# A table set loaded by hand, a clamp moved to VectorE, and a re-timed plan in an attention and two-MLP kernel

## The chip, the cores and the metric

One core of a Trainium2 chip runs the whole program. The metric is the device time of one execution in microseconds, the median of several; lower is better.

## The reference

Three layers follow each other. Delta-rule attention keeps a 48x48 state per head, for 4 batches, 8 heads and 768 steps; its output, seen as 3072 tokens of 384, goes through a first Mlp with a rational function, and then through a second Mlp with Mish. Both Mlps have 2048 hidden units, and their weights come as float64.

```python
for t in range(S):
    y[:, :, t] = einsum('bhd,bhde->bhe', q_t, state)
    v_old = einsum('bhde,bhd->bhe', state, k_t)          # k_t is normalised
    state = state + b_t * einsum('bhd,bhe->bhde', k_t, v_t - v_old)
h = x @ w_in;  P = a0 + a1*h + a2*h**2 + a3*h**3
Q = 1 + |b0|*|h| + |b1|*h**2;  x = (P / (Q + 1e-6)) @ w_out     # first Mlp
h = x @ w_in2; out = (h * tanh(log1p(exp(h)))) @ w_out2           # second Mlp (Mish)
```

## The kernel before

**Stages.** Time is cut into 24 chunks of 32 steps, and four chunks make a group G of 512 tokens (G from 0 to 5). A group passes through: norms of k (`norms`), per chunk transposes and Gram products on PE (`prepare`), one triangular inverse for all four chunks (`inverse`: a VectorE transpose at L355, 30 elimination steps of a product L364 and a sum L370, a transpose back L374, a scaling L377), and four recurrent steps (`step`, one chunk each, whose second product at L431 needs the inverse `xt`). The inverse's 30 steps run on VectorE for G = 0 and on GpSimd (POOL) for G = 1 to 5 (`ONPOOL`). Then come 16 units of the first Mlp and 16 of the second, each unit a slice of 128 hidden columns: nine matmuls up (L639), an elementwise chain, nine matmuls down (L645). The stages follow one another as first Mlp G0, second Mlp G0, first G1, second G1, first G2, second G2, first G3, second G3, first G4, first G5, second G4, second G5. The steps of group G + 1 lie beside the second Mlp of group G, so the stage pairs carry attention work as well.

**The first Mlp's unit.** On ScalarE (ACT) it runs Abs (L665), Identity (L669, every other unit; else POOL does it at L667), Identity (L670), Ln (L674), Exp (L675) and a copy (L679); the quotient 1/Q is exp(-ln Q), improved by a Newton step on VectorE (DVE: L672, L673, L676 to L678). POOL multiplies at L671 and forms the low half at L680. The hidden tile `h` has two PSUM banks, so the up product of unit i + 2 waits until the chain of unit i has read its bank, at L673 last. The second Mlp's unit has two Mish activations (L682, L683) and one DVE subtraction (L684).

**Function tables.** One preload at the start of the program (L746) selects a set that holds both Ln and Exp. Everywhere else the table load in front of an activation is put there when the program is compiled, not by this code; it is seen in the trace as ACT_TABLE_LOAD with the line of the activation behind it.

**Weights.** 64 tiles of float64 weights (16 slices, two sides, two Mlps) are turned into pairs of float32 tiles and stored in a scratch in HBM, from which each unit fetches its slice (L632). A tile j goes through a load into `raw` (L532 to L543), a magnitude into `wm` (L549 on ACT, or L547 on DVE for the last 20), a clamp (L552), a shift, a sign and a low part on DVE (L557, L562, L567), a high half on ACT (L574), a low half on POOL (L577) and a store (L590). The clamp is on POOL for j below 24 and from 44 on, on DVE between. `raw`, `wm` and `st` have two buffers each.

**The plan.** No engine's order is written out. `Plan.add` takes every operation with an engine, a planned duration in ns, and the buffers that it reads and writes; `Plan.order` works back from the units' due times to a latest start of every operation, takes the operation's `early` off it, and then simulates the engines in time: whenever one is free it takes, among its operations that are ready, the one with the smallest value. The code is issued in that order, and each engine, and SP's queue of DMA issues with it, runs its own part strictly in that order. So planned durations and `early` values change no instruction, only the order; `AHEADX` is the `early` of the norms, of the copies and masks of `prepare` and of the whole inverse, and 0 before.

Of the kernel before, what the change touches and what calls it, by code (L numbers as in the profile page):

```python
# [23 lines left out]
START = 90000  # L24
AHEAD = 30000
AHEADP = 100000
AHEADX = 0
ONPOOL = (1, 2, 3, 4, 5)
LAG = 3.5
EARLY = 6  # L30
PER_KB = 3.3


# [93 lines left out]
class Attention:  # L127
# [222 lines left out]
    def inverse(self, p, G):  # L350
        nc, M, tmp, xt, xs = self.nc, self.M, self.tmp, self.xt, self.xs
        engine, eng = ("POOL", nc.gpsimd) if G in ONPOOL else ("DVE", nc.vector)

        def first():
            nc.vector.transpose(out=xs, in_=self.lg.rearrange("p u m s -> p s (u m)"))  # L355

        def diag():
            eng.memset(xs.rearrange("p a b -> p (a b)")[:, 0:C * C:C + 1], 1.0)

        def step(j):  # L360
            def f():
                n = C - 1 - j
                tv = tmp[:, 0:j * n].rearrange("p (c i) -> p c i", c=j)
                eng.tensor_tensor(  # L364
                    out=tv,
                    in0=xs[:, j, j + 1:C].unsqueeze(1).to_broadcast([128, j, n]),
                    in1=xs[:, 0:j, j:j + 1].to_broadcast([128, j, n]),
                    op=ALU.mult,
                )
                eng.tensor_tensor(out=xs[:, 0:j, j + 1:C], in0=xs[:, 0:j, j + 1:C], in1=tv, op=ALU.add)  # L370
            return f

        def last():
            nc.vector.transpose(out=xt.rearrange("p n t -> p t n"), in_=xs.rearrange("p j i -> p i j"))  # L374

        def scale():
            nc.gpsimd.tensor_tensor(  # L377
                out=xt, in0=xt,
                in1=self.beta_t[:, GU * G:GU * G + GU].rearrange("p u m -> p (u m)").unsqueeze(2).to_broadcast([128, GU * M, C]),
                op=ALU.mult,  # L380
            )

        p.add("DVE", 2000, first, [f"lg{g}" for g in range(GU)], ["xs"], early=AHEADX)
        p.add(engine, 160, diag, (), ["xs"], early=AHEADX)
        for j in range(1, C - 1):
            n = j * (C - 1 - j)
            p.add(engine, int(3.4 * n + 440) if engine == "POOL" else 2 * (n + 190), step(j), (), ["xs", "tmp"], early=AHEADX)
        p.add("DVE", 2070, last, ["xs"], ["xt"], early=AHEADX)
        p.add("POOL", 1950, scale, (), ["xt"], early=AHEADX)

    def step(self, p, u):
        nc, M, D = self.nc, self.M, self.D
# [100 lines left out]

        p.dma(8 * 400, 300, lambda: self.load_v(u), (), [vb], early=AHEAD)
        p.dma(1200, 200, swap, [knb], [knsb], early=AHEAD)
        p.add("PE", 850, ks, [kb, f"{sb}0", f"{sb}1"], [bc], early=AHEAD)
        p.add("DVE", 560, rest, [bc, vb], ["r2"], early=AHEAD)
        p.add("PE", 850, uu, ["r2", "xt"], [bc], early=AHEAD)
        p.add("ACT", 480, u_out, [bc], ["U"], early=AHEAD)
        if u + 1 < self.NU:  # L500
            for c in range(2):
                p.add("PE", 850, s_mm(c), ["U", knb, knsb], [bs[c]], early=AHEAD)
                p.add("DVE", 560, s_out(c), [bs[c], f"{sb}{c}"], [f"{tb}{c}"], early=AHEAD)
        p.add("PE", 2600, y_mm, [f"{sb}0", f"{sb}1", "U", qb, ab], [by], early=AHEAD)
# [6 lines left out]
class Weights:  # L511
# [8 lines left out]
        self.w_in = w_in  # L520
        self.w_out = w_out.rearrange("f (k c) -> f k c", c=128)

    def plan(self, p, f, side, j, late, pool):
        nc, bufs = self.nc, self.bufs
        raw, m, st = (bufs[n][j % len(bufs[n])] for n in ("raw", "wm", "st"))
        rawb, mb, stb = (f"{n}{j % len(bufs[n])}" for n in ("raw", "wm", "st"))
# [22 lines left out]
                nc.scalar.activation(out=m.bitcast(F32), in_=words[:, :, 1].bitcast(F32), func=ACTF.Abs)  # L549

        def size():
            (nc.gpsimd if pool else nc.vector).tensor_scalar(  # L552
                out=m.bitcast(F32), in0=m.bitcast(F32), scalar1=self.LEAST, scalar2=self.MOST, op0=ALU.max, op1=ALU.min,
            )

# [22 lines left out]

        p.dma(380 if side or self.n else 2500, 384, get, (), [rawb])
        if late:  # L580
            p.add("DVE", 600, mag, [rawb], [mb])
        else:
            p.add("ACT", 550, mag, [rawb, "table"], [mb])
        p.add("POOL" if pool else "DVE", 720 if pool else 450, size, (), [mb])
        p.add("DVE", 450, shift, (), [mb])
        p.add("DVE", 650, sign, [rawb], [mb])
        p.add("DVE", 650, low, [rawb], [mb])
        p.add("ACT", 510, hi, [mb], [stb])
        p.add("POOL", 1040, lo, [mb], [stb])
        p.dma(380, 384, lambda: nc.sync.dma_start(out=self.scratch[f][:, side], in_=st.bitcast(F32)), [stb], [f"wd{self.n}_{f}_{side}"])  # L590


class Mlps:
# [22 lines left out]
    def plan_unit(self, p, m, G, NG, f, nf, due):  # L616
# [41 lines left out]

        p.dma(330, 384, fetch(0, win), [f"wd{m - 1}_{f}_0"], [winb], early=6000)
        p.dma(330, 384, fetch(1, wout), [f"wd{m - 1}_{f}_1"], [woutb], early=6000)  # L660
        p.add("PE", 2050, up, [winb] + [f"X{b}_{j}" for j in range(GU)], [hb], due=due)
        act = nc.scalar.activation
        V, A, P = nc.vector, nc.scalar, nc.gpsimd
        if m == 1:
            p.add("ACT", 595, lambda: act(out=q, in_=h, func=ACTF.Abs), [hb], [qb])  # L665
            if i % 2:
                p.add("POOL", 810, lambda: P.tensor_scalar(out=r, in0=q, scalar1=k["b1"], scalar2=k["b0"], op0=ALU.mult, op1=ALU.add), [qb], [rb])  # L667
            else:
                p.add("ACT", 820, lambda: act(out=r, in_=q, func=ACTF.Identity, scale=k["b1"], bias=k["b0"]), [qb], [rb])  # L669
            p.add("ACT", 775, lambda: act(out=s, in_=h, func=ACTF.Identity, scale=k["a3"], bias=k["a2"]), [hb], [sb])  # L670
            p.add("POOL", 1335, lambda: P.tensor_tensor(out=q, in0=q, in1=r, op=ALU.mult), [rb], [qb])  # L671
            p.add("DVE", 680, lambda: V.tensor_tensor(out=s, in0=s, in1=h, op=ALU.mult), [hb], [sb])  # L672
            p.add("DVE", 750, lambda: V.scalar_tensor_tensor(out=s, in0=s, scalar=k["a1"], in1=h, op0=ALU.add, op1=ALU.mult), [hb], [sb])  # L673
            p.add("ACT", 2000 if first and G in (1, 2, 3, 4) else 690, lambda: act(out=r, in_=q, func=ACTF.Ln, bias=k["c"]), [qb], [rb] + (["table"] if first and G in (1, 2, 3, 4) else []))  # L674
            p.add("ACT", 580, lambda: act(out=rp, in_=r, func=ACTF.Exp, scale=-1.0), [rb, "table"], ["r"])  # L675
            p.add("DVE", 685, lambda: V.scalar_tensor_tensor(out=q, in0=q, scalar=1.0 + 1e-6, in1=rp, op0=ALU.add, op1=ALU.mult), ["r"], [qb])  # L676
            p.add("DVE", 750, lambda: V.scalar_tensor_tensor(out=rp, in0=s, scalar=k["a0"], in1=rp, op0=ALU.add, op1=ALU.mult), [sb], ["r"])  # L677
            p.add("DVE", 690, lambda: V.scalar_tensor_tensor(out=q, in0=q, scalar=2.0, in1=rp, op0=ALU.subtract, op1=ALU.mult, reverse0=True), ["r"], [qb])  # L678
            p.add("ACT", 625, lambda: A.copy(out=gh[:, 0], in_=q), [qb], [ghb])  # L679
            p.add("POOL", 1320, lambda: P.tensor_tensor(out=gh[:, 1], in0=q, in1=gh[:, 0].bitcast(F32), op=ALU.subtract), [qb], [ghb])  # L680
        else:
            p.add("ACT", 2000 if first and G < 5 else 600, lambda: act(out=gh[:, 0], in_=h, func=ACTF.Mish), [hb], [ghb] + (["table"] if first and G < 5 else []))  # L682
            p.add("ACT", 595, lambda: act(out=q, in_=h, func=ACTF.Mish), [hb, "table"], [qb])  # L683
            p.add("DVE", 700, lambda: V.tensor_tensor(out=gh[:, 1], in0=q, in1=gh[:, 0].bitcast(F32), op=ALU.subtract), [qb], [ghb])  # L684
        if m == 2 and G == NG - 1:
            rows = ["o0", "o1", "o2", "t0"]
            p.add("PE", 2100, down_rows, [woutb, ghb], rows, due=due + LAG * PACE)
# [36 lines left out]
def tile_delta_attention_two_mlps(  # L724
# [120 lines left out]
```

## Time and profile before

| | us |
|---|---|
| median of 3 runs (1470.32 to 1471.16) | 1470.34 |
| the profiled execution's own time | 1469.16 |
| its span, first to last instruction | 1467.4 |

| engine | busy, us | share of the span |
|---|---|---|
| PE (TensorE matmul) | 1139.7 | 78% |
| ACT (ScalarE) | 787.8 | 54% |
| DVE (VectorE) | 701.3 | 48% |
| POOL (GpSimd) | 635.2 | 43% |

Busy time is the time in which at least one instruction of the engine was running. A stage is a stretch between the first up products of two neighbouring groups of 16 units, read from the starts of L639. The granted clock is TensorE's clock as a share of full speed, so a PE that is busy at a low clock does less.

### The profile page before, as it was taken

How to read it: one execution, taken by the hardware profiler on the slowest of the kernel's cores; microseconds unless marked ns; L12 is line 12 of the kernel's file. 1: busy time of each engine (PE TensorE's matmuls, PEld its weight loads, DVE VectorE, ACT ScalarE, POOL GpSimd, SP SyncE). 2: the span in 40 equal slices, each digit the busy share in tenths (PEclk: the TensorE clock that was granted, in tenths of full speed). 3: DMA queues.
4: the chain of work that ended last, by engine and by line, in shares of the span. 5: the costliest groups of instructions: out<-in, count | busy, mean ns of one | idle time of the engine just before them, and what ended most of it. 6: DMA issues, size and time to landing. Idle time of an engine off the chain costs nothing.

```text
span 1467.4 us, 32391 instructions
## 1 busy us (share of the span) xinstructions
PE 1139.7 (78%) x13162; PEld 898.4 (61%) x13162; DVE 701.3 (48%) x1128; ACT 787.8 (54%) x1177; POOL 635.2 (43%) x743
## 2 busy tenths in 40 slices
PE   5048766578877778997788978889984897789986
PEld 4047544356665656775566766667763675568776
DVE  4874889776535542236632236532142655552211
ACT  2123665422258971259961279942273889992211
POOL 5453765696425573015672025770038434440000
PEclk9556988788888999998999998999997899999998
DMA  5755777766783644554644546553543344547562
GB/s 114 201 167 133 234 222 240 235 198 214 212 241 84 197 110 127 130 152 112 183 131 115 140 119 167 144 148 99 130 113 96 83 110 133 134 134 192 160 197 76
DMA packets 209285, 224.81 MB, mean 153 GB/s; under 512 B 134864, under 2 KB 147664, under 8 KB 209136
## 3 DMA queue, kind: packets, MB, share of 16 engines
q1 hardware_dynamic: 205616, 222.04, 54.6%
q8 instruction: 104, 1.70, 0.5%
q10 hardware_dynamic: 3264, 0.59, 0.2%
q14 instruction: 45, 0.37, 0.1%
q0 software_dynamic: 256, 0.10, 0.0%
HBM read 190.42 MB, written 29.88 MB: 150 GB/s over the span
## 4 chain that ended last, share of the span: by engine, by line
PE 31%; ACT 31%; POOL 13%; DVE 7%; DMA 6%; issue 6%; SPq 5%; ACTq 0%; DVEq 0%; POOLq 0%
PE b_h L639 11%; PE b_o L645 9%; ACT L675 6%; ACT L674 6%; POOL xs L370 5%; POOL tmp L364 4%; ACT mr L674 4%; ACT ms L670 3%; ACT b_r L675 3%; ACT mq L665 3%; ACT gh L679 2%; PE b_t L448 2%; SPq L712 2%; POOL wm L552 2%; DMA raw<-in_moe_w_in_dram 2%
## 5 line engine op out<-in xcount | busy, mean ns | idle before, releaser
L639 PE MATMUL b_h<-x,win 128*128 128x512 f32 x1728 | 478.4, 427 | 109.8 <-DVE ms L673 91.3
L645 PE MATMUL b_o<-gh,wout 128*128 128x512 f32 x1584 | 430.1, 418 | 61.6 <-POOL gh L680 27.5
L639 PEld LDWEIGHTS b_h<-x,win 128*128 128x128 f32 x1728 | 344.4, 205 | 204.1 <-DVE ms L673 106.7
L645 PEld LDWEIGHTS b_o<-gh,wout 128*128 128x128 f32 x1584 | 309.0, 201 | 146.5 <-POOL gh L680 38.5
L682 ACT ACTIVATE gh<-b_h 128x512 fp32r<-128x512 f32 x96 | 57.4, 598 | 264.5 <-PE b_h L639 258.9
L680 POOL TENSOR_TENSOR gh<-mq,gh 128x512 fp32r<-128x512 f32 x96 | 123.2, 1285 | 134.2 <-ACT gh L679 131.6
L671 POOL TENSOR_TENSOR mq<-mq,mr 128x512 f32<-128x512 f32 x96 | 125.0, 1303 | 101.8 <-ACT mr L669 90.0
L684 DVE TENSOR_TENSOR gh<-mq,gh 128x512 fp32r<-128x512 f32 x96 | 72.1, 754 | 178.6 <-ACT mq L683 176.2
L676 DVE SCALAR_TENSOR_TENSOR mq<-mq,b_r 128x512 f32<-128x512 f32 x96 | 65.9, 686 | 188.4 <-ACT b_r L675 179.2
L335 POOL TENSOR_TENSOR mb<-beta_t,mask 128x256 f32<-128x256 f32 x24 | 15.5, 647 | 233.8 <-DVE lg L325 233.6
L674 ACT ACT_TABLE_LOAD x77 | 98.8, 1283 | 1.4
L675 ACT ACT_TABLE_LOAD x77 | 98.8, 1283 | 1.4
L552 POOL TENSOR_SCALAR wm<-wm 128x384 f32<-128x384 f32 x44 | 66.8, 1519 | 70.9 <-ACT wm L549 46.6
L577 POOL TENSOR_TENSOR st<-wm,st 128x384 fp32r<-128x384 f32 x64 | 67.7, 1063 | 58.9 <-ACT st L574 58.4
L672 DVE TENSOR_TENSOR ms<-ms,b_h 128x512 f32<-128x512 f32 x96 | 65.5, 682 | 53.1 <-ACT ms L670 53.0
L370 POOL TENSOR_TENSOR xs<-xs,tmp 128x30 f32<-128x30 f32 (+9 forms) x150 | 83.9, 559 | 11.8
L431 PE MATMUL b_t<-r,xt 32*32 32x48 f32 x1536 | 26.0, 226 | 71.3 <-POOL xt L377 71.3
L364 POOL TENSOR_TENSOR tmp<-xs 128x30 f32<-128x30 f32 (+9 forms) x150 | 76.9, 512 | 8.6
L665 ACT ACTIVATE mq<-b_h 128x512 f32<-128x512 f32 x96 | 56.5, 588 | 41.8 <-PE b_h L639 24.4
L670 ACT ACTIVATE ms<-b_h,ab 128x512 f32<-128x512 f32 x96 | 73.6, 767 | 5.2 <-DVE b_r L677 5.1
L674 ACT ACTIVATE mr<-mq,cst 128x512 f32<-128x512 f32 x96 | 69.0, 722 | 7.9 <-POOL mq L671 7.0
L673 DVE SCALAR_TENSOR_TENSOR ms<-ms,ab,b_h 128x512 f32<-128x512 f32 x96 | 71.4, 744 | 2.5 <-ACT mq L665 0.7
(128 smaller groups left out, 1548.0 us busy)
## 6 DMA issues: line engine op xcount, KB each, us to landing
win<-wd SPq DMA_DIRECT2D x192, 384.0 KB
wout<-wd SPq DMA_DIRECT2D x192, 384.0 KB
wd<-st SPq DMA_DIRECT2D x64, 384.0 KB
raw<-in_moe_w_out_dram SPq DMA_DIRECT2D x32, 384.0 KB
raw<-in_moe_w_in_dram SPq DMA_DIRECT2D x16, 384.0 KB
v<-in_v_dram SPq DMA_DIRECT2D x192, 24.0 KB
qn<-in_q_dram SPq DMA_DIRECT2D x92, 48.0 KB
kn<-in_k_dram SPq DMA_DIRECT2D x88, 48.0 KB
```

What stands on the lines that cost most here:

```text
L364: eng.tensor_tensor(out=tv, in0=xs[:, j, j + 1:C].unsqueeze(1).to_broadcast([128, j, n]), in1=xs[:, 0:j, j:j + 1].to_broadcast([128, j, n] ...
L370: eng.tensor_tensor(out=xs[:, 0:j, j + 1:C], in0=xs[:, 0:j, j + 1:C], in1=tv, op=ALU.add)
L552: (nc.gpsimd if pool else nc.vector).tensor_scalar(out=m.bitcast(F32), in0=m.bitcast(F32), scalar1=self.LEAST, scalar2=self.MOST, op0=ALU. ...
L639: nc.tensor.matmul(out=h, lhsT=win[:, a, j], rhs=x[:, c, slab[j]], start=n == 0, stop=n == 8)
L645: nc.tensor.matmul(out=self.banks[f"o{d}"], lhsT=wout[:, a, d], rhs=gh[:, c], start=first and j == 0, stop=last and j == 2,)
L665: p.add("ACT", 595, lambda: act(out=q, in_=h, func=ACTF.Abs), [hb], [qb])
L670: p.add("ACT", 775, lambda: act(out=s, in_=h, func=ACTF.Identity, scale=k["a3"], bias=k["a2"]), [hb], [sb])
L671: p.add("POOL", 1335, lambda: P.tensor_tensor(out=q, in0=q, in1=r, op=ALU.mult), [rb], [qb])
L674: p.add("ACT", 2000 if first and G in (1, 2, 3, 4) else 690, lambda: act(out=r, in_=q, func=ACTF.Ln, bias=k["c"]), [qb], [rb] + (["table"] ...
L675: p.add("ACT", 580, lambda: act(out=rp, in_=r, func=ACTF.Exp, scale=-1.0), [rb, "table"], ["r"])
L680: p.add("POOL", 1320, lambda: P.tensor_tensor(out=gh[:, 1], in0=q, in1=gh[:, 0].bitcast(F32), op=ALU.subtract), [qb], [ghb])
L684: p.add("DVE", 700, lambda: V.tensor_tensor(out=gh[:, 1], in0=q, in1=gh[:, 0].bitcast(F32), op=ALU.subtract), [qb], [ghb])
```

## The change

- In front of the Ln of the first unit of the first Mlp, for G = 1 to 4, the set with Ln and Exp is loaded by an instruction of the kernel's own.
- The weights' clamp is on DVE for all 64 tiles (44 move from POOL).
- `raw` and `wm` get a third buffer each.
- `AHEADX` goes from 0 to 40000, so the norms, the copies of `prepare` and the inverse are ordered as if they were due 40 us sooner.
- Planned durations are set anew; these are the ones changed:

```diff
-AHEADX = 0
+AHEADX = 40000
...
+RAW = 3
+WM = 3
...
-        p.add("POOL", 1950, scale, (), ["xt"], early=AHEADX)
+        p.add("POOL", 2300, scale, (), ["xt"], early=AHEADX)
...
-        p.add("PE", 850, ks, [kb, f"{sb}0", f"{sb}1"], [bc], early=AHEAD)
+        p.add("PE", 885, ks, [kb, f"{sb}0", f"{sb}1"], [bc], early=AHEAD)
...
-                p.add("PE", 850, s_mm(c), ["U", knb, knsb], [bs[c]], early=AHEAD)
+                p.add("PE", 1140, s_mm(c), ["U", knb, knsb], [bs[c]], early=AHEAD)
...
-        p.add("PE", 2600, y_mm, [f"{sb}0", f"{sb}1", "U", qb, ab], [by], early=AHEAD)
+        p.add("PE", 1700, y_mm, [f"{sb}0", f"{sb}1", "U", qb, ab], [by], early=AHEAD)
...
-            (nc.gpsimd if pool else nc.vector).tensor_scalar(
+            nc.vector.tensor_scalar(
...
-            p.add("DVE", 600, mag, [rawb], [mb])
+            p.add("DVE", 400, mag, [rawb], [mb])
...
-        p.add("POOL" if pool else "DVE", 720 if pool else 450, size, (), [mb])
+        p.add("DVE", 400, size, (), [mb])
...
-        p.add("PE", 2050, up, [winb] + [f"X{b}_{j}" for j in range(GU)], [hb], due=due)
+        p.add("PE", 2080, up, [winb] + [f"X{b}_{j}" for j in range(GU)], [hb], due=due)
...
+            def log():
+                if first and G in (1, 2, 3, 4):
+                    A.preload_act_table_set("natural_log_exp_and_others")
+                act(out=r, in_=q, func=ACTF.Ln, bias=k["c"])
...
-        "raw": [const.tile([128, 3, 128], I64, name=f"raw{i}") for i in range(2)],
-        "wm": [const.tile([128, 384], I32, name=f"wm{i}") for i in range(2)],
+        "raw": [const.tile([128, 3, 128], I64, name=f"raw{i}") for i in range(RAW)],
+        "wm": [const.tile([128, 384], I32, name=f"wm{i}") for i in range(WM)],
```

The other planned durations move by 5% or less, but for the subtraction at L684 (700 to 755) and the transpose at L705 (1050 to 710).

## Rows read from the trace of the kernel before

**Rows 1.** The page: the span, and the chain that ended last by engine.

```profile
span 1467.4 us, 32391 instructions
...
PE 31%; ACT 31%; POOL 13%; DVE 7%; DMA 6%; issue 6%; SPq 5%; ACTq 0%; DVEq 0%; POOLq 0%
```

**Rows 2.** Stages: stretch, length, busy of PE, PEld, DVE, ACT, POOL; clock; DMA share, GB/s.

```profile
0.00:139.00 139.00, 62.98 (x1763) 55.52 (x1763) 84.67 (x172) 36.97 (x76) 64.68 (x86) 0.69 0.61 158
139.00:277.20 138.20, 92.89 (x563) 69.32 (x561) 114.83 (x181) 79.92 (x143) 88.51 (x76) 0.83 0.73 222
277.20:425.90 148.70, 112.42 (x1538) 87.39 (x1535) 86.28 (x135) 41.50 (x79) 93.90 (x108) 0.82 0.72 221
425.90:542.20 116.30, 90.44 (x653) 68.93 (x652) 63.59 (x100) 105.95 (x136) 64.66 (x76) 0.91 0.51 136
542.20:644.10 101.90, 94.52 (x1603) 74.45 (x1602) 25.88 (x42) 27.88 (x53) 22.95 (x36) 0.97 0.54 139
644.10:754.00 109.90, 85.38 (x585) 64.63 (x584) 61.06 (x97) 101.64 (x131) 63.14 (x73) 0.94 0.51 135
...
855.80:965.80 110.00, 87.39 (x586) 67.13 (x584) 61.16 (x97) 101.70 (x131) 63.21 (x73) 0.91 0.51 136
...
1070.80:1210.30 139.50, 106.96 (x1619) 82.14 (x1616) 66.44 (x101) 99.00 (x131) 77.33 (x103) 0.87 0.38 97
1210.30:1301.50 91.20, 69.78 (x272) 53.02 (x270) 52.24 (x76) 87.47 (x114) 41.48 (x36) 0.94 0.49 133
```

**Rows 3.** Waits of PE: engine, line, releaser; us in total, times, longest us.

```profile
PE b_h L639 <- DVE ms L673: 91.3, 37, 7.1
PE b_t L431 <- POOL xt L377: 71.3, 4, 52.1
```

**Rows 4.** Line L674: ns min/median/max, first and last start in us; two kinds.

```profile
L674 ACT ACTIVATE mr<-mq,cst x96: 705/723/727, 148.7 to 1310.0; 128x512 f32<-128x512 f32 x96
L674 ACT ACT_TABLE_LOAD  x77: 1283/1283/1283, 430.8 to 1308.7; - x77
```

**Rows 5.** Groups of the run: busy us, mean ns, idle before.

```profile
L675 ACT ACT_TABLE_LOAD x77 | 98.8, 1283 | 1.4
```

**Rows 6.** Groups of ACT in the first Mlp of G5, 1210.3 to 1301.5 us.

```profile
L674 ACT ACT_TABLE_LOAD x15 | 19.2, 1283 | 0.3
```

**Rows 7.** Weights: the clamp on either engine, and the shift behind it (as Rows 4).

```profile
L552 POOL TENSOR_SCALAR wm<-wm x44: 1487/1488/1795, 19.9 to 420.1; 128x384 f32<-128x384 f32 x44
L552 DVE TENSOR_SCALAR wm<-wm x20: 297/360/1098, 193.2 to 292.1; 128x384 f32<-128x384 f32 x20
...
L557 DVE TENSOR_SCALAR wm<-wm x64: 350/362/2067, 21.4 to 421.6; 128x384 int32<-128x384 int32 x64
```

**Rows 8.** Waits of SP's queue in the second Mlp of G0, 277.2 to 425.9 us.

```profile
SPq L590 <- POOL st L577: 21.5, 14, 3.6
SPq L534 <- DVE wm L567: 14.4, 7, 3.4
```

**Rows 9.** The inverse of G0 on DVE, in order of time: start us, us, line.

```profile
39.10 1.93 DVE L355 STREAM_TRANSPOSE xs<-lg 128x1024 f32<-128x1024 f32 x1
...
86.34 2.05 DVE L374 STREAM_TRANSPOSE xt<-xs 128x1024 f32<-128x1024 f32 x1
```

**Rows 10.** Groups of the run: the inverse's steps on DVE (G0) and on POOL (G1 to G5).

```profile
L370 POOL TENSOR_TENSOR xs<-xs,tmp 128x30 f32<-128x30 f32 (+9 forms) x150 | 83.9, 559 | 11.8
...
L364 POOL TENSOR_TENSOR tmp<-xs 128x30 f32<-128x30 f32 (+9 forms) x150 | 76.9, 512 | 8.6
...
L370 DVE TENSOR_TENSOR xs<-xs,tmp 128x30 f32<-128x30 f32 (+14 forms) x30 | 11.7, 392 | 1.0
...
L364 DVE TENSOR_TENSOR tmp<-xs 128x30 f32<-128x30 f32 (+14 forms) x30 | 11.3, 376 | 0.8
```

**Rows 11.** Groups of the run: the first Mlp's two long POOL operations.

```profile
L671 POOL TENSOR_TENSOR mq<-mq,mr 128x512 f32<-128x512 f32 x96 | 125.0, 1303 | 101.8 <-ACT mr L669 90.0 <-PE b_o L645 6.3 <-DMA qn<-in_q_dram 1.6
L680 POOL TENSOR_TENSOR gh<-mq,gh 128x512 fp32r<-128x512 f32 x96 | 123.2, 1285 | 134.2 <-ACT gh L679 131.6 <-DVE ms L672 1.7 <-DMA win<-wd 0.9
```

More of the change, by code (lines that the diff above doesn't have):

```diff
@@ L495, in step @@
         p.dma(1200, 200, swap, [knb], [knsb], early=AHEAD)
-        p.add("PE", 850, ks, [kb, f"{sb}0", f"{sb}1"], [bc], early=AHEAD)
+        p.add("PE", 885, ks, [kb, f"{sb}0", f"{sb}1"], [bc], early=AHEAD)
         p.add("DVE", 560, rest, [bc, vb], ["r2"], early=AHEAD)
-        p.add("PE", 850, uu, ["r2", "xt"], [bc], early=AHEAD)
+        p.add("PE", 885, uu, ["r2", "xt"], [bc], early=AHEAD)
         p.add("ACT", 480, u_out, [bc], ["U"], early=AHEAD)
@@ L501, in step @@
             for c in range(2):
-                p.add("PE", 850, s_mm(c), ["U", knb, knsb], [bs[c]], early=AHEAD)
+                p.add("PE", 1140, s_mm(c), ["U", knb, knsb], [bs[c]], early=AHEAD)
                 p.add("DVE", 560, s_out(c), [bs[c], f"{sb}{c}"], [f"{tb}{c}"], early=AHEAD)
-        p.add("PE", 2600, y_mm, [f"{sb}0", f"{sb}1", "U", qb, ab], [by], early=AHEAD)
+        p.add("PE", 1700, y_mm, [f"{sb}0", f"{sb}1", "U", qb, ab], [by], early=AHEAD)
         p.add("ACT", 480, y_out, [by], [yb], early=AHEAD)
-        p.add("PE", 800, x_mm, [yb], [bx], early=AHEAD)
+        p.add("PE", 890, x_mm, [yb], [bx], early=AHEAD)
         p.add("ACT", 490, x_hi, [bx], [xb], early=AHEAD)
@@ L521, in __init__, with plan @@
         self.w_out = w_out.rearrange("f (k c) -> f k c", c=128)
-    def plan(self, p, f, side, j, late, pool):
+    def plan(self, p, f, side, j, late):
         nc, bufs = self.nc, self.bufs
@@ L580, in plan @@
         if late:
-            p.add("DVE", 600, mag, [rawb], [mb])
+            p.add("DVE", 400, mag, [rawb], [mb])
         else:
             p.add("ACT", 550, mag, [rawb, "table"], [mb])
-        p.add("POOL" if pool else "DVE", 720 if pool else 450, size, (), [mb])
-        p.add("DVE", 450, shift, (), [mb])
-        p.add("DVE", 650, sign, [rawb], [mb])
-        p.add("DVE", 650, low, [rawb], [mb])
+        p.add("DVE", 400, size, (), [mb])
+        p.add("DVE", 430, shift, (), [mb])
+        p.add("DVE", 640, sign, [rawb], [mb])
+        p.add("DVE", 640, low, [rawb], [mb])
         p.add("ACT", 510, hi, [mb], [stb])
-        p.add("POOL", 1040, lo, [mb], [stb])
+        p.add("POOL", 1060, lo, [mb], [stb])
         p.dma(380, 384, lambda: nc.sync.dma_start(out=self.scratch[f][:, side], in_=st.bitcast(F32)), [stb], [f"wd{self.n}_{f}_{side}"])
@@ L673, in plan_unit @@
             p.add("DVE", 750, lambda: V.scalar_tensor_tensor(out=s, in0=s, scalar=k["a1"], in1=h, op0=ALU.add, op1=ALU.mult), [hb], [sb])
-            p.add("ACT", 2000 if first and G in (1, 2, 3, 4) else 690, lambda: act(out=r, in_=q, func=ACTF.Ln, bias=k["c"]), [qb], [rb] + (["table"] if first and G in (1, 2, 3, 4) else []))
+            p.add("ACT", 2000 if first and G in (1, 2, 3, 4) else 720, log, [qb], [rb] + (["table"] if first and G in (1, 2, 3, 4) else []))
             p.add("ACT", 580, lambda: act(out=rp, in_=r, func=ACTF.Exp, scale=-1.0), [rb, "table"], ["r"])
@@ L683, in plan_unit @@
             p.add("ACT", 595, lambda: act(out=q, in_=h, func=ACTF.Mish), [hb, "table"], [qb])
-            p.add("DVE", 700, lambda: V.tensor_tensor(out=gh[:, 1], in0=q, in1=gh[:, 0].bitcast(F32), op=ALU.subtract), [qb], [ghb])
+            p.add("DVE", 755, lambda: V.tensor_tensor(out=gh[:, 1], in0=q, in1=gh[:, 0].bitcast(F32), op=ALU.subtract), [qb], [ghb])
         if m == 2 and G == NG - 1:
@@ L693, in plan_unit @@
             return
-        p.add("PE", 2050, down, [woutb, ghb], ["o0", "o1", "o2"], due=due + LAG * PACE)
+        p.add("PE", 2080, down, [woutb, ghb], ["o0", "o1", "o2"], due=due + LAG * PACE)
         if not last:
@@ L704, in plan_unit @@
                 ev, evb = self.ev[d % 2], f"ev{d % 2}"
-                p.add("DVE", 1050, lambda ev=ev, o=o: V.transpose(out=ev, in_=o), [f"o{d}"], [evb], due=due + (LAG + 2) * PACE)
+                p.add("DVE", 710, lambda ev=ev, o=o: V.transpose(out=ev, in_=o), [f"o{d}"], [evb], due=due + (LAG + 2) * PACE)
                 for n in range(TOK // 32):
@@ L792, in tile_delta_attention_two_mlps @@
             for side in range(2):
-                ws[n].plan(plan, f, side, j, n == 1 and f >= EARLY, j < 24 or j >= 2 * (NF + EARLY))
+                ws[n].plan(plan, f, side, j, n == 1 and f >= EARLY)
                 j += 1
```

## The prediction

> **What bounds the kernel now.** I read the page first: over the span [rows 1] the chain that ended last is PE and ACT in equal parts, 31% each, with 13% on POOL, so no engine bounds the whole and the stages have to be told apart. The table of stages [rows 2] does that. The reader is to look in each row for the engine whose busy time comes nearest to the stretch's length. In the five first-Mlp stages after G0's (the two rows from 425.90 and 644.10, the one from 855.80, and the two from 1070.80 and 1210.30) it is ACT: 105.95 of 116.30, 101.64 of 109.90, 101.70 of 110.00, 99.00 of 139.50, 87.47 of 91.20. In a later second-Mlp stage (from 542.20) it is PE, 94.52 of 101.90, which is 93%, at a granted clock of 0.97 (near the 2.4 GHz level). The two stages from 139.00 and 277.20 are nobody's: DVE has 83% in the first, PE 76% in the second at a clock of only 0.82, and the DMA engines 0.73 and 0.72, more than anywhere later. There the float64 weights are converted.
>
> Next the waits of PE say what it lacks: 91.3 us for L673, the last reader of a hidden bank, in 37 waits, and 71.3 us for the inverse `xt` in 4 waits, of which one is 52.1 [rows 3]. The view of line L674 then shows why ACT is full: the first units' Ln, from 148.7 us on, have no load in front; from 430.8 on there are 77 table loads of 1283 ns for the 80 Ln of G1 to G5 [rows 4], and the Exp behind them has another 77 [rows 5]. The last first-Mlp stage shows it undiluted, with 15 loads at L674 [rows 6] and, as they come in pairs with those of L675, about 29 in all: 29 x 1.283 = 37 us of a stage of 91.20.
>
> **The change part by part.** The sum is made against the profiled execution's own time, 1469.2 us (span 1467.4 and 1.8 around it); the median of the runs is 1.2 us above that.
>
> *The table set, loaded by hand.* In G0 a hand-loaded set serves Ln and Exp of 16 units with no load between them [rows 4], so the 154 loads go: 154 x 1.283 = 197.6 us of ACT. The four hand loads cost nothing more, as each stands where a load stands now. ACT in the stage from 425.90 falls from 105.95 by 32 x 1.283 = 41 to 65 us, in the last from 87.47 to about 50. Not all of that is time: PE is next, with 90.44, 85.38, 87.39, 106.96 and 69.78 us of work. What is late next is the up product, which waits for L673, and that line's own queue: DVE has 63.59 of work, POOL 64.66 in such a stage, both below PE. PE's work gets shorter too, because its clock was 0.91, 0.94, 0.91, 0.87 and 0.94 while it kept stopping; I scale it to 0.96. Then I take PE to be busy for 90% of a stage, a little under the 93% of the row from 542.20, since a first-Mlp unit is the longer chain; 85% for the stage from 1070.80, which is the slackest now and holds an inverse and four steps; 95% for the last, which holds no attention work. This makes 95.3, 92.9, 92.0, 114.0 and 71.9 us in place of 116.3, 109.9, 110.0, 139.5 and 91.2: 21.0 + 17.0 + 18.0 + 25.5 + 19.3 = 101 us gained. The low end: clock as now and 85% everywhere, 106.4, 100.4, 102.8, 125.8 and 82.1, gains 49. The high end: 0.97 and 93% (97% in the last), gains 125. I stay near the high end because the row from 542.20 is the nearest of all: the same matmuls beside steps, with ACT free.
>
> Of a load's price the rows say 1283 ns and no more: in the last such stage ACT is idle for 91.20 - 87.47 = 3.7 us in all [rows 2]. The Trainium skill, ScalarE: Activation LUTs, "What ACT_TABLE_LOAD costs", adds a drain of about 1380 ns to every load, by which 154 loads would hold ACT for an estimated 410 us; here 15 loads at L674 alone would need 20.7 us of drain, so the trace agrees with the 1283 ns and not with the drain.
>
> *The inverse 40 us earlier.* Three of PE's four waits for `xt` share 71.3 - 52.1 = 19.2 us, at the head of later second-Mlp stages [rows 3]. An earlier order removes them (the copies and squares of the norms and of `prepare` move up on ACT with it, and lie beside an ACT that has 41 us to spare a stage), but the first-Mlp stage in front gets shorter by some 20 us and the inverse's 32 us on POOL (160.8 us for five [rows 10]) stays; I take 10, with 0 and 19 as ends.
>
> *The weights.* Four things go together here, up to the start of the stage from 425.90.
> First, G0's inverse: 60 steps of 23.0 us in all [rows 10] lie between 41.0 and 86.3 us [rows 9], 45 us, with conversion work among them and DVE waiting for POOL's clamp. With 40 us of priority they can close up, and the first units may start up to 20 us sooner.
> Second, the clamp: 1488 ns on POOL against 360 on DVE [rows 7], so a tile's way is 1.1 us shorter, 44 tiles take 44 x 1.49 = 65 us off POOL and put 44 x 0.36 = 16 us on DVE.
> Third, the third `raw` and `wm`: SP's queue waits in that stage 14.4 us for a `raw` to be read (L534) [rows 8], and the fetches of the units (L632) and the loads of v queued behind that issue wait with it. With a third buffer the load can be issued a tile sooner; nothing is issued more often, so SP's queue gets no longer. `st` keeps two, so the 21.5 us for the low half [rows 8] stay, cut only by a freer POOL.
> Fourth, what the rows set as limits: DMA at 0.73 and 0.72 over 286.9 us would need 231 us at 0.90, a gain of 56 at most; DVE's 114.83 leaves 23 us of the stage from 139.00; the stage from 277.20 can't fall below its twin from 542.20, 46.8 us less.
> So the ends are 0 (the pace of the tiles is set by DVE and DMA as now, and an earlier start only waits longer for weights) and 20 + 56 = 76. I take 50: 15 for the start and 35 for the pace, above the middle, as two of the three waits in a tile's way are shortened at once.
>
> A clamp on DVE can be slowed by POOL beside it: its longest is 1098 ns against a median of 360, and the shift behind it goes up to 2067 [rows 7]. The Trainium skill, SBUF — State Buffer, "SBUF: two separate sides", says that a DVE operation that uses two ports and a GpSimd operation exclude each other for a whole instruction; no row counts how many of those long ones are due to it. By that rule every moved clamp could wait for an operation of 1.3 us on POOL [rows 11], 44 x 1.3 = 57 us more on DVE, and the pace would gain nothing.
>
> *The plan's durations.* They add no work; the order of all queues changes. No row prices that; the ends are 15 us either way (about the 7.4 us that PE idles in the stage from 542.20, twice), taken as 0.
>
> Sum: 101 + 10 + 50 = 161; 1469.2 - 161 = 1308, and 1.2 for the median: **1309 us**.
>
> **The rivals.** *The weights keep their pace* (DVE or the DMA engines as the bound of the conversion). For it: DVE at 83% and DMA at 0.73 [rows 2], and 16 us more on DVE. Against: SP's waits for `raw` [rows 8]. The 50 go: 1359, from 1340 to 1385.
> *PE fills everywhere*: all high ends, 125 + 19 + 76 = 220, gives 1250. Against: even the calmest row leaves 7% idle.
> *The hand load doesn't hold*, and loads come back in front of Ln and Exp: then only 60 are gained, 1410. Against: G0 [rows 4].
> *The earlier inverse blocks POOL* (slower than before). POOL runs its queue in order. If the plan puts the 60 steps of an inverse in one piece ahead of L671 and L680, units stop, and with two hidden banks PE stops two units later. Each inverse is 160.8 / 5 = 32.2 us [rows 10], five of them 161, and the low halves of the weights queue behind the first, so the 50 go as well: 1469.2 - 111 + 161 + 1.2 = 1520. It decides from 111 / 5 = 22 us of stop per inverse. For it: the priority of 40 us is about that of nine units at their planned 4.2 us. Against: the two POOL operations take 1303 and 1285 ns a unit [rows 11], and 64.66 us of POOL work fit in a stage of 95.
>
> **How the numbers follow.** The forecast has 0.65, with 1280 to 1345 as its own range (loads 80 to 120, weights 35 to 65, not all at one end); the weights keeping their pace 0.20; PE filling 0.08; the hand load failing 0.03; POOL blocking 0.04, of which 0.01 is for a stop that just cancels the gain. A measurement of this kernel tells some 0.2% (2.9 us) from no change. So faster is 0.65 + 0.20 + 0.08 + 0.03 = 0.96, same 0.01, slower 0.03. The range 1262 to 1375 takes in the forecast, most of the first rival, and a corner of the second; about 0.17 is left out.
>
> **What would show it.** Right: no loads at L675 and four at L674; first-Mlp stages of 92 to 95 us with PE at 90% and a clock of 0.95 or more; the waits for `xt` in later stages gone or below 4 us; the stage at 425.90 starting near 376, with DMA shares above 0.8 before it and the 23 us of G0's inverse in under 30. Wrong: PE waiting for L680 or L671 with inverse steps on POOL in front (blocking); PE waiting for `win` or `wout` and the early stages as long as now with DVE over 85% (the first rival); loads still counted at L675.

## The result, and the profile after

The changed kernel takes 1344.18 us (median of 4, 1342.18 to 1345.09), the one before 1470.75 beside it: a ratio of 0.9133, 95% interval 0.9117 to 0.915. That is 126.6 us less, where 161 were forecast. The page of the changed kernel (span, busy time of the engines, and the chain that ended last by engine) answers to [rows 1] and the table of engines:

```profile
span 1340.5 us, 32163 instructions
...
PE 1098.8 (82%) x13168; PEld 873.9 (65%) x13168; DVE 713.5 (53%) x1172; ACT 586.1 (44%) x1022; POOL 570.8 (43%) x699
...
PE 45%; POOL 10%; DVE 9%; DMA 6%; SPq 6%; ACT 5%; issue 3%; DVEq 0%; POOLq 0%; ACTq 0%
```

ACT has lost 787.8 - 586.1 = 201.7 us of work and has all but left the chain, from 31% to 5%; PE went from 31% to 45%. All lines moved by the diff: up is L641 now, down L647, Ln L670 with its hand load at L669, Exp L682, the copy L686, the low half L687, the bank's last reader L680, the clamp L554, the inverse L366 and L372. The groups of table loads (count, busy us, mean ns, idle before) answer to [rows 4, 5]:

```profile
L689 ACT ACT_TABLE_LOAD x7 | 9.0, 1283 | 0.1
L672 ACT ACT_TABLE_LOAD x4 | 5.1, 1283 | 4.6 <-PE b_h L641 4.6
L669 ACT ACT_TABLE_LOAD x4 | 5.1, 1283 | 0.1
L753 ACT ACT_TABLE_LOAD x1 | 1.3, 1283 | 0.8 <-PEq L837 0.8
L551 ACT ACT_TABLE_LOAD x1 | 1.3, 1283 | 0.0
```

Of the 154 loads in front of Ln and Exp none is left, but for the four by hand. The stages (columns as in [rows 2]):

```profile
0.00:113.30 113.30, 61.94 (x1760) 54.76 (x1760) 68.87 (x161) 28.63 (x59) 30.77 (x60) 0.74 0.55 129
113.30:264.60 151.30, 97.14 (x571) 69.43 (x568) 133.78 (x198) 83.96 (x154) 92.08 (x92) 0.82 0.76 231
264.60:409.60 145.00, 108.93 (x1742) 83.07 (x1742) 98.73 (x178) 48.71 (x91) 61.59 (x75) 0.87 0.81 252
409.60:500.80 91.20, 79.62 (x443) 62.73 (x443) 62.75 (x96) 61.10 (x99) 70.51 (x85) 0.94 0.61 170
...
983.00:1113.00 130.00, 98.82 (x1737) 76.13 (x1736) 66.30 (x102) 63.01 (x104) 78.59 (x103) 0.88 0.39 105
1113.00:1178.70 65.70, 65.52 (x289) 53.95 (x288) 53.09 (x80) 52.71 (x89) 43.33 (x38) 1.00 0.69 188
```

The reader is to see three things here. In the rows from 409.60 and 1113.00 PE is now the engine nearest to the length, in the last one all of it, at a clock of 1.00 (the 2.4 GHz level). The row from 983.00 is still 31 us longer than its PE work. And the two stages of G0, from 113.30 and 264.60, are together 296.3 us, where they were 286.9 before: the first units start 25.7 us sooner, and only 16.3 of that reach the first stage of G1. Summed over the stages, as the starts of the up products give them:

| us | before | changed | load alone |
|---|---|---|---|
| up to the first stage of G1 | 425.9 | 409.6 | 422.7 |
| first Mlp, G1 to G5 | 566.9 | 467.6 | 446.5 |
| second Mlp, G1 to G5 | 474.6 | 463.3 | 471.3 |
| span | 1467.4 | 1340.5 | 1340.5 |

The last column is the first experiment. PE's waits, which answer to [rows 3]:

```profile
PE b_h L641 <- DVE ms L680: 42.6, 21, 6.7
PE b_o L647 <- POOL gh L687: 41.4, 13, 27.0
PE b_t L433 <- POOL xt L379: 39.3, 3, 25.7
...
PE b_h L641 <- DMA raw<-in_moe_w_in_dram: 14.8, 1, 14.8
```

The wait for the hidden bank has halved (91.3 to 42.6); of what is left, 33.2 lie in the first Mlp of G0, where it was 25.7 before. Of the wait for the inverse `xt`, 25.7 us are G0's own start, and 39.3 - 25.7 = 13.6 lie in two of the later second Mlps; before, it was 19.2 in three. Two other single waits stand out, of 27.0 us (the longest for a low half was 11.8 before) and of 14.8. The first is the inverse of G5, in one piece on POOL. The order of time on POOL, and then on PE (start us, us):

```profile
1010.65 0.24 POOL L366 TENSOR_TENSOR tmp<-xs 128x30 f32<-128x30 f32 x1
...
1044.93 0.27 POOL L372 TENSOR_TENSOR xs<-xs,tmp 128x30 f32<-128x30 f32 x1
1045.14 2.53 POOL L687 TENSOR_TENSOR gh<-mq,gh 128x512 fp32r<-128x512 f32 x2
...
1046.47 3.78 PE L647 MATMUL b_o<-gh,wout 128*128 128x512 f32 x8 [27.00 <-POOL gh L687]
```

Sixty steps run from 1010.65 to 1045.2 with no unit's work between them, then the low half L687 that a down product has waited for. In three stretches of that stage PE works with gaps, then stands, and then hardly stops at all:

```profile
983.00:1019.47 36.47, 32.42 (x375) 24.42 (x373) 25.38 (x40) 24.56 (x39) 19.23 (x30) 0.95 0.41 97
1019.47:1046.47 27.00, 0.00 (x0) 0.00 (x0) 2.73 (x4) 0.38 (x2) 23.72 (x44) 0.58 0.28 89
1046.47:1113.00 66.53, 66.40 (x1362) 51.70 (x1363) 38.19 (x60) 38.07 (x65) 35.65 (x30) 0.96 0.43 115
```

The second, the 14.8 us, ends at 289.1, before the third unit's up product in the second Mlp of G0; on ACT:

```profile
274.36 0.60 ACT L689 ACTIVATE gh<-b_h 128x512 fp32r<-128x512 f32 x1 [0.45 <-PE b_h L641]
274.97 1.28 ACT L551 ACT_TABLE_LOAD   x1
...
286.07 0.55 ACT L551 ACTIVATE wm<-raw 128x384 f32<-128x384 f32 x1 [1.90 <-DMA raw<-in_moe_w_out_dram]
286.64 1.28 ACT L689 ACT_TABLE_LOAD   x1
287.94 0.60 ACT L689 ACTIVATE gh<-b_h 128x512 fp32r<-128x512 f32 x1
```

The plan lets only the first unit's first Mish wait for all the weights' Abs (they share the plan's buffer `table`), so another unit's Mish went ahead of it at 274.36, and the rest had to wait for the last Abs and its raw weights, at the price of two more loads. The kernel before had the same, with 9.3 us of wait up to 292 us.

### The profile page after: what moved, and what is told of

Read it like the earlier page. It is cut to its first block, busy times and chain, and to the rows that moved or that the text cites. A ratio compares the mean times of both kernels' runs of the same rounds, so it can differ in the third digit from the quotient of the medians.

```text
span 1340.5 us, 32163 instructions
## 1 busy us (share of the span) xinstructions
PE 1098.8 (82%) x13168; PEld 873.9 (65%) x13168; DVE 713.5 (53%) x1172; ACT 586.1 (44%) x1022; POOL 570.8 (43%) x699
## 4 chain that ended last, share of the span: by engine, by line
PE 45%; POOL 10%; DVE 9%; DMA 6%; SPq 6%; ACT 5%; issue 3%; DVEq 0%; POOLq 0%; ACTq 0%
PE b_h L641 18%; PE b_o L647 17%; SPq L719 4%; POOL xs L372 4%; POOL tmp L366 3%; PE b_t L450 3%; PE b_t L469 2%; DMA wd<-st 2%; DMA win<-wd 2%; DMA raw<-in_moe_w_in_dram 1%; PE b_t L433 1%; PE b_o L656 1%; POOL gh L687 1%; DVE b_r L684 1%; DMA out_dram<-ev 1%
## 5 line engine op out<-in xcount | busy, mean ns | idle before, releaser
L641 PE MATMUL b_h<-x,win 128*128 128x512 f32 x1728 | 461.5, 415 | 79.2 <-DVE ms L680 42.6
L647 PE MATMUL b_o<-gh,wout 128*128 128x512 f32 x1584 | 417.8, 411 | 66.2 <-POOL gh L687 41.4
L641 PEld LDWEIGHTS b_h<-x,win 128*128 128x128 f32 x1728 | 334.6, 198 | 165.0 <-DVE ms L680 50.8
L647 PEld LDWEIGHTS b_o<-gh,wout 128*128 128x128 f32 x1584 | 302.7, 196 | 145.2 <-POOL gh L687 49.2
L687 POOL TENSOR_TENSOR gh<-mq,gh 128x512 fp32r<-128x512 f32 x96 | 125.1, 1304 | 65.2 <-ACT gh L686 51.0
L372 POOL TENSOR_TENSOR xs<-xs,tmp 128x30 f32<-128x30 f32 (+9 forms) x150 | 82.0, 547 | 11.8
L670 ACT ACTIVATE mr<-mq,cst 128x512 f32<-128x512 f32 x96 | 69.1, 721 | 29.1 <-POOL mq L678 28.8
L366 POOL TENSOR_TENSOR tmp<-xs 128x30 f32<-128x30 f32 (+9 forms) x150 | 77.6, 518 | 8.6
L680 DVE SCALAR_TENSOR_TENSOR ms<-ms,ab,b_h 128x512 f32<-128x512 f32 x96 | 71.2, 742 | 1.7
L684 DVE SCALAR_TENSOR_TENSOR b_r<-ms,ab,b_r 128x512 f32<-128x512 f32 x96 | 71.8, 748 | 0.0
L682 ACT ACTIVATE b_r<-mr 128x512 f32<-128x512 f32 x96 | 57.5, 599 | 28.8 <-DVE mq L685 27.7
L576 ACT CAST st<-wm 128x384 fp32r<-128x384 f32 x64 | 32.3, 509 | 80.4 <-DVE wm L569 48.6
L686 ACT CAST gh<-mq 128x512 fp32r<-128x512 f32 x96 | 58.7, 612 | 19.3 <-DVE mq L685 19.0
```

What stands on the lines that cost most here:

```text
L366: eng.tensor_tensor(out=tv, in0=xs[:, j, j + 1:C].unsqueeze(1).to_broadcast([128, j, n]), in1=xs[:, 0:j, j:j + 1].to_broadcast([128, j, n] ...
L641: nc.tensor.matmul(out=h, lhsT=win[:, a, j], rhs=x[:, c, slab[j]], start=n == 0, stop=n == 8)
L647: nc.tensor.matmul(out=self.banks[f"o{d}"], lhsT=wout[:, a, d], rhs=gh[:, c], start=first and j == 0, stop=last and j == 2,)
```

## The experiments

Each ran beside the kernel before; intervals are 95%. The first two ask what the table loads are worth, from either side.

**Load alone.** The kernel before with the function `log` of the diff in place of the lambda at L674, and nothing else.

> The kernel before with the hand load alone. Theory (the 99 us that the first-Mlp stages of G1 to G5 got shorter come from the table loads): 1471 - 99 = about 1372 us, with the start of the first G1 stage where it was, near 426 us. If the inverse in one piece on POOL is a cost of the 40 us priority, the first Mlp of G4 gains more here than in the changed kernel (139.5 to below 125 us) and the total may go down to 1360. Rival (the new order is needed to turn freed ACT time into time): 1400 us or more.

Measured: 1345.09 us, ratio 0.9153 (0.9127 to 0.9179). The one part gives as much as the whole change (0.9117 to 0.915), against both expectations. Stages of its trace:

```profile
422.70:512.80 90.10, 82.63 (x653) 65.39 (x652) 62.34 (x100) 62.66 (x103) 63.46 (x74) 0.96 0.63 178
...
992.20:1114.80 122.60, 99.28 (x1616) 75.98 (x1617) 67.05 (x102) 64.66 (x105) 78.11 (x103) 0.92 0.41 110
1114.80:1176.20 61.40, 61.40 (x272) 50.59 (x271) 50.38 (x76) 50.13 (x85) 42.16 (x36) 1.00 0.68 193
```

The first-Mlp stages get 566.9 - 446.5 = 120 us shorter, not 99. In the last of them PE never stops, at a clock of 1.00. The first Mlp of G4 takes 122.6, below the 125 that the theory named; here units' work lies among the steps of the inverse of G5, and the longest wait for a low half is 14.8 us.

**All but the load.**

```diff
-                if first and G in (1, 2, 3, 4):
-                    A.preload_act_table_set("natural_log_exp_and_others")
```

> The changed kernel without the hand load; Ln and Exp get their loads back. Theory (the parts add): 1344 + 99 = about 1443 us, stages of G1 to G3 at 110 us or more. Rival (the other parts hold a share of the 99): 1425 us or less.

Measured: 1456.83 us, ratio 0.9913 (0.9889 to 0.9937). So the other four parts give 0.9% without the load, and with it nothing that can be told from none. The stages of G1 to G3 are 108.9, 116.2 and 115.6 us, about as the theory had it, but the total is 14 us above its 1443: the first-Mlp stages of G1 to G5 sum to 576.6, so in this order the load takes 109 us off them, not 99.

**AHEADX back at 0.**

```diff
-AHEADX = 40000
+AHEADX = 0
```

> The changed kernel with AHEADX back at 0. Theory (the priority helps the first start but holds the weights back, and puts the inverse of G5 in one piece in front of POOL's unit work, 27 us of PE's time): first units start 15 to 25 us later than 113, the first G1 stage starts no later than 410, the first Mlp of G4 is 15 to 27 us shorter, later second-Mlp stages get 5 us longer each; in all 1325 to 1340 us. Rival (the priority is a clear gain): 1360 us or more.

Measured: 1334.63 us, ratio 0.9079 (0.9052 to 0.9106): faster than the changed kernel, and the theory's total. The first stage of G1 starts at 409.1, as expected. The other parts were not: the first units start at 122, only 9 us later; the first Mlp of G4 still takes 126.1, with 21.8 us of wait for L687, as 48 of the 60 steps of the inverse of G5 stand in one piece on POOL without the priority, too; and the second-Mlp stages of G1 to G5 sum to 460.1, 3 us less than with the priority, not more.

**Two buffers.**

```diff
-RAW = 3
-WM = 3
+RAW = 2
+WM = 2
```

> The changed kernel with two buffers each for raw and wm. Theory (the third buffer carries the faster pace of the weights, 5.3 us a tile against 6.3): first G1 stage starts 20 to 40 us later than 410, total 1365 to 1385 us. Rival (DVE, at 88% in the first Mlp of G0, sets the pace whatever the buffers): within 6 us of 1344.

Measured: 1370.39 us, ratio 0.9317 (0.9281 to 0.9354); the first stage of G1 starts at 433.7, both as expected. In this kernel the third buffer is worth 26 us.

**Third buffer on the load alone.** The first experiment's kernel with `range(3)` for `raw` and `wm`.

> The kernel before with the hand load and the third raw and wm buffers, and nothing else (AHEADX 0, clamp on POOL for 44 tiles, durations of before). Theory (the third buffer is worth about 26 us wherever it is put, and the other three parts cost what it gives): 1320 to 1328 us, the fastest so far. Rival (the third buffer only repairs what the priority of the inverse does to the weights): 1338 us or more.

Measured: 1345.72 us, ratio 0.9168 (0.914 to 0.9195). The rival: with AHEADX at 0, the clamp on POOL and the durations of before, the same buffer is worth nothing. The first units start at 118.0, 15 us sooner than with the load alone, but the first stage of G1 at 423.2, where it was 422.7. That the buffer only repairs what the priority does is not shown by it, as the parts don't add. Two other runs add to this kernel the clamp on DVE and one thing more: with the new durations it is the run above with AHEADX at 0 (0.9079), with the priority the run below with the durations of before (0.909). Either is faster than this one, the intervals apart; with both, in the changed kernel, more than half of that is lost again (0.9133).

**Clamp on POOL again**, for the 44 tiles of before.

```diff
-            nc.vector.tensor_scalar(
+            (nc.gpsimd if pool else nc.vector).tensor_scalar(
...
-        p.add("DVE", 400, size, (), [mb])
+        p.add("POOL" if pool else "DVE", 720 if pool else 400, size, (), [mb])
```

> The changed kernel with the clamp on POOL for 44 tiles again. The load alone gave 1345 us and everything together 1344, though the third buffer is worth 26 and AHEADX costs 10, so clamp and durations together should cost about 15. Theory (DVE, at 88% of the first Mlp stage of G0, sets the weights' pace, and 16 us of clamps and more on it are the cost): 1325 to 1335 us, DVE below 85% there. Rival (the cost lies in the new durations): 1344 us or more, as POOL's 1488 ns is back in every tile's way.

Measured: 1342.13 us, ratio 0.9145 (0.9105 to 0.9185), the first stage of G1 at 410.1. No difference: neither 1.1 us in a tile's way nor 16 us of DVE tell.

**Durations of before.** All planned durations set back, among them `y_mm` to 2600, `s_mm` to 850, `mag` to 600.

> The changed kernel with the planned durations of before (the clamp on DVE at 450). Theory (the order from the new durations is worse): 1325 to 1335 us, with the first-Mlp stages of G1 to G5 nearer to those of the load alone (446 us in all, against 467 in the changed kernel). Rival (durations closer to the trace are a gain or nothing): 1340 us or more.

Measured: 1333.29 us, ratio 0.909 (0.9053 to 0.9127), against 0.9117 to 0.915: the intervals just overlap. The first-Mlp stages of G1 to G5 sum to 453.7, 14 less than in the changed kernel and 7 more than with the load alone. So beside the priority the new durations gained nothing; that they cost some 10 us there is likely and not certain.

The next four ask what sets the pace of the weights in the two stages of G0.

**A third of the raw weights**, in the same order.

```diff
-                nc.sync.dma_start(out=raw, in_=self.w_out[cols])
+                if j < 4:
+                    nc.sync.dma_start(out=raw, in_=self.w_out[cols])
+                else:
+                    nc.sync.dma_start(out=raw[:, 0], in_=self.w_out[cols, 0])
...
-                nc.sync.dma_start(out=raw, in_=self.w_in.rearrange("(k p) f -> p k f", p=128)[:, :, cols])
+                nc.sync.dma_start(out=raw[:, 0], in_=self.w_in.rearrange("(k p) f -> p k f", p=128)[:, 0, cols])
```

> The changed kernel in the same order, but for 46 of the 64 tiles only a third of the raw weights is loaded (the rest of the tile holds older data), about 12 MB of the 83 MB of the early stages. If the DMA engines set the weights' pace (share 0.76 and 0.81): the first G1 stage starts 25 to 45 us earlier than 410, total 1300 to 1320 us. If DVE sets it: within 8 us of 1344.

Measured: 1329.18 us, ratio 0.9061 (0.9023 to 0.9098); its stages are shown with the next run's.

**No clamp**, in the same order.

```diff
-        p.add("DVE", 400, size, (), [mb])
+        p.add("DVE", 400, lambda: None, (), [mb])
```

> The changed kernel in the same order with the clamp left out of all 64 tiles: 64 x 0.36 to 0.5 = 23 to 32 us less on DVE and some 0.5 us less in each tile's way. If DVE sets the weights' pace: the first G1 stage starts 15 to 30 us earlier than 410, total 1315 to 1330 us. If the DMA engines set it: within 8 us of 1344.

Measured: 1328.92 us, ratio 0.9055 (0.8995 to 0.9115). The two stages of G0, first of the kernel with a third of the raw weights:

```profile
110.40:258.70 148.30, 97.56 (x568) 70.83 (x568) 133.24 (x201) 85.14 (x155) 93.72 (x94) 0.85 0.67 205
258.70:402.50 143.80, 113.61 (x1743) 87.19 (x1743) 102.09 (x178) 47.60 (x91) 61.75 (x75) 0.83 0.66 205
```

and then of the kernel without the clamp:

```profile
110.80:260.40 149.60, 103.65 (x569) 74.29 (x569) 121.41 (x175) 84.23 (x154) 92.91 (x92) 0.80 0.77 236
260.40:403.40 143.00, 108.59 (x1743) 83.67 (x1742) 82.14 (x147) 47.51 (x90) 60.11 (x75) 0.86 0.80 249
```

In the one the DMA share falls from 0.76 and 0.81 to 0.67 and 0.66, in the other DVE's work from 133.78 and 98.73 us to 121.41 and 82.14; the stages stay within 3 us of 151.3 and 145.0, and the first stage of G1 starts 7 and 6 us sooner (402.5, 403.4). Neither the bytes nor DVE's work alone sets the pace. Of the 12 and 14 us that each span is shorter, the rest lies in later stages, where nothing was left out, and is no part of the answer.

**Half of the weights.** The second Mlp's tiles aren't converted.

```diff
-    for n in range(2):
+    for n in range(1):
         for f in range(NF):
...
-            return lambda: nc.sync.dma_start(out=w.bitcast(F32), in_=self.wd[m - 1][f][:, side])
+            return lambda: nc.sync.dma_start(out=w.bitcast(F32), in_=self.wd[0][f][:, side])
```

> The changed kernel without the conversion of the second Mlp's 32 tiles; its units fetch the first Mlp's weights instead, and the order is planned anew. Less DVE work and fewer DMA bytes alone moved the first G1 stage by 7 us. Theory (the way of each tile through five queues, in an order shared with the units, sets the pace of the two early stages): with half of the tiles gone the second Mlp of G0 falls from 145 to about its later twins' 97 to 105 us, and the first G1 stage starts near 340; total about 1275 us. Rival (the two stages are held by the attention work beside them, the inverse and steps of G1): 2nd Mlp of G0 stays above 125 us, total above 1310.

Measured: 1288.11 us, ratio 0.8775 (0.8754 to 0.8796). The two stages of G0:

```profile
110.30:256.40 146.10, 96.05 (x568) 69.73 (x569) 120.16 (x188) 80.17 (x144) 85.17 (x88) 0.83 0.74 224
256.40:357.70 101.30, 92.92 (x1599) 73.46 (x1598) 27.09 (x40) 27.90 (x53) 30.25 (x47) 0.97 0.54 141
```

The second is as short as its later twins, beside the same inverse and steps; the first, which still has its own weights, stayed at 146, so the next stage starts at 357.7, not near 340.

**Four tiles.** As above with `range(2)` slices converted and `self.wd[0][f % 2]` fetched.

> The changed kernel with only 4 of the 64 weight tiles converted (two slices of the first Mlp), which all units of both Mlps fetch in turn; the order is planned anew. Theory (the ordered way of the tiles sets the first Mlp stage of G0 too, not DVE's or the DMA engines' amount of work): that stage falls from 151 to 85 to 100 us, the waits of PE for the last reader of the hidden bank there fall from 33 us to below 12, the second Mlp of G0 stays at 97 to 105, total about 1225 us. Rival (the attention work of G1 beside it, its Gram products and its inverse, holds the stage): it stays above 120 us.

Measured: 1226.0 us, ratio 0.8353 (0.8299 to 0.8407). The two stages of G0, and PE's wait for the bank in the first:

```profile
112.60:188.20 75.60, 73.11 (x563) 58.70 (x562) 60.71 (x97) 58.50 (x98) 62.84 (x73) 1.00 0.67 184
188.20:288.30 100.10, 93.56 (x1604) 73.98 (x1603) 27.60 (x42) 27.98 (x53) 23.53 (x38) 0.97 0.54 140
...
PE b_h L641 <- DVE ms L680: 1.9, 1, 1.9
```

The theory, and more: 151.3 falls to 75.6 us, below the 85 to 100 expected. The converted weights cost the changed kernel 1344 - 1226 = 118 us, all of it in these two stages; the start at 112.6 doesn't move, so that is the attention's own.

**The last inverse on DVE.**

```diff
-ONPOOL = (1, 2, 3, 4, 5)
+ONPOOL = (1, 2, 3, 4)
```

> The changed kernel with the inverse of G5 on DVE in place of POOL. Theory (the inverse in one piece, 35 us on POOL in front of the low halves of the first Mlp of G4, costs PE its 27 us wait): that wait goes, the stage falls from 130 to 105 to 118 us, total 1320 to 1332 us. Rival (PE waits for the chain of G5's steps at the end of the stage anyway, so the 27 us only move there): the stage stays at 125 us or more, total within 6 us of 1344.

Measured: 1339.51 us, ratio 0.9118 (0.9097 to 0.9139), no difference that can be told. The first Mlp of G4 takes 131.6 us, and PE waits there for another thing:

```profile
PE b_t L433 <- POOL xt L379: 25.0, 1, 25.0
```

The wait for the low half became a wait for `xt`. Its stage in three stretches, as above:

```profile
977.60:1011.40 33.80, 28.92 (x376) 22.39 (x370) 21.12 (x39) 22.09 (x35) 14.67 (x15) 1.00 0.46 110
1011.40:1036.40 25.00, 0.00 (x0) 0.00 (x0) 23.18 (x58) 0.72 (x1) 2.90 (x2) 0.54 0.25 75
1036.40:1109.20 72.80, 69.64 (x1372) 54.71 (x1373) 42.11 (x67) 40.17 (x68) 29.06 (x25) 0.95 0.39 108
```

The inverse is done 59 us into the stage, where it was 67, but the planned order now has less of PE's work ahead of the stop and more behind it. So the total fits the rival, and its reason does not: PE does not wait at the end of the stage, and G5's last step ends near 1100, 9 us before the next stage begins. The stop belongs to the inverse, on POOL or on DVE, and to the little work that PE has been given ahead of it.

## Why the prediction was right, and where it was not

The time lies in the range, and the direction and the main mechanism are shown: taking the loads away is worth 0.0847 of the time alone. It is 35 us above the forecast of 1309, though, and only 15 below the first rival's 1359; the step that failed is the weights' pace. By the steps:

*The table loads*: 101 us over five stages were forecast; 99 came in the changed kernel. By stage 25.1, 22.3, 17.0, 9.5 and 25.4 for the 21.0, 17.0, 18.0, 25.5 and 19.3 of the sum. PE took over nearly as said (87% at 0.94 in the row from 409.60, for 90% at 0.96). That the total came out so close is luck, as two errors cancel: the load alone gives 120, near the high end of 125, and the new order took 21 back; with the durations of before 14 of these 21 return.

*The row from 1070.80 at 85%* is the mis-sized part of that term, 9.5 us for 25.5. The prediction counted this row among those where ACT is nearest to the length, with 99.00 of 139.50, but PE's 106.96 was nearer, so the loads had the least to give here. And it sized the stage by a share of PE; what the share misses is one stop of 27.0 us, behind which PE is full (66.40 of 66.53). With the inverse on DVE the stop is still 25.0 us, so it is not POOL's blocking alone; why the order leaves PE so little ahead of it stays open.

*The inverse 40 us earlier*: 10 us were forecast, from the waits for `xt` at the heads of later second-Mlp stages. Those stages are 474.6 - 463.3 = 11.3 us shorter, but that is luck, too. One of the three waits went (5.6 us, in the second Mlp of G1) and two stay, 13.6 us, where the prediction wanted them gone or below 4 each. Another 6.3 us of the 11.3 lie in a stage without an inverse, here before and after:

```profile
1301.50:1373.10 71.60, 69.63 (x298) 56.81 (x299) 20.65 (x30) 32.20 (x51) 7.61 (x7) 0.98 0.65 178
1178.70:1244.00 65.30, 65.30 (x289) 54.07 (x288) 18.08 (x27) 23.70 (x43) 5.17 (x5) 1.00 0.69 194
```

And without the priority the five stages sum to even less, 460.1. The whole part costs in this kernel: without it, it is faster (0.9052 to 0.9106 against 0.9117 to 0.915). Its price was looked for on POOL alone.

*The weights*, 50 us: 16.3 came. This is the step that failed, and in it the pace: for the 15 us of the start 25.7 came, for the 35 of the pace -9.4 (286.9 to 296.3 us in the two stages). "Above the middle, as two of the three waits in a tile's way are shortened at once" was the wrong choice between 0 and 76. G0's inverse did close up, from 45 to 22 us (it runs from 39.4 to 61.4), and the start came above even the 20 allowed for. But what went first held the weights back: seven tiles were stored by 105 us where before it were twelve by 101. With two buffers the first stage of G1 starts at 433.7, later than before; the third buffer brings it to 409.6, and the moved clamp changed nothing. The low end's mechanism, an earlier start that only waits longer for weights, was the better description: with AHEADX at 0 the first units start 9 us later, and the first stage of G1 at 409.1 all the same. The limits read from busy shares were no limits either: DVE and DMA, each with 9% or more of its work taken out, moved the stages by 3 us at most. With hardly any weights the stages fall to their twins' length or below (75.6 and 100.1 us), so it is the conversion that holds them. Whether its pace comes from the order in which five in-order queues take a tile's parts among the units' work, or from DVE and DMA binding in turn, stays open.

*A clamp slowed by POOL*: the clamp and the shift behind it in the changed kernel (ns min/median/max) answer to [rows 7]:

```profile
L554 DVE TENSOR_SCALAR wm<-wm x64: 344/361/2005, 23.8 to 397.8; 128x384 f32<-128x384 f32 x64
L559 DVE TENSOR_SCALAR wm<-wm x64: 351/361/1420, 24.6 to 398.9; 128x384 int32<-128x384 int32 x64
```

The medians stay, and the longest are as long as before, on the other one of the two. So the exclusion of which the Trainium skill, SBUF — State Buffer, "SBUF: two separate sides", speaks may be in these tails, but in the run with the clamp on POOL no cost of it can be told.

*The plan's durations*: taken as 0 within 15. Beside the priority they cost about 10 us, inside the bound; with AHEADX at 0 they and the clamp gain about as much (0.9079 against 0.9168). A term for each part alone, as in the sum, has no place for this.

*The rivals*: the weights kept their pace, or lost some, as the first rival had it, and its sign is there: both early stages as long as before, DVE at 133.78 of 151.30 (88%) in the first, PE's waits for `win` at 17.5 us (8.7 before). Its reason, DVE or DMA as the bound, is borne out for neither alone by the runs with less of its work. The 1344 lies in its range (1340 to 1385) and, at the very end, in the forecast's (1280 to 1345). The inverse did block POOL, once, for 27.0 us near the price of 32.2, but with the inverse on DVE PE stopped about as long; 22 us a stop in every stage, the point from which it would have decided, was never near.

## What to carry to other kernels

When a change has several parts, the part that removes work from the bounding engine can be all of the gain: here one hand-placed load did what five edits did together. The others don't add: either the priority or the new durations, with the clamp, took 11 to 12 us off the kernel with load and buffers, and both together nothing that can be told, so parts that only change an order are to be tried together as well as one by one. A stage of the table whose longest engine is busy 75 to 88% of it is not yet explained by any of them; leave out some of one engine's work, and then all of the stage's extra work, before an end of the range is chosen from such shares. A wait that ends at an in-order queue's big block is worth fixing only if the block itself is not what the stage needs next.

## What the runs showed of the hardware

A table load took 1283 ns with no idle time of note in front of it (0.1 us over the four by hand). Where PE hardly stopped for a whole stage its granted clock was 1.00, the 2.4 GHz level (65.52 us of 65.70 in the changed kernel, 61.40 of 61.40 with the load alone); in the row from 113.30, where it was busy for 97.14 of 151.30 in pieces, it was 0.82, and in the 27.0 us without any work 0.58, near the 1.2 GHz level. So the loads' removal paid twice in the last first-Mlp stage: with the load alone PE's own work there fell from 69.78 us, at a clock of 0.94, to 61.40. The clock would give 69.78 x 0.94 = 65.6; what gave the other 4 us no run shows.
